# A state-space mixer with product-key experts: joint tap bursts, 16-bit column sums, and a fold remainder made once for two heads

## The chip, the cores and the metric

The kernel runs on one core of a Trainium2 chip. Its metric is the device time of one execution in microseconds (us), here the median of three runs. Five engines work side by side: TensorE (PE, with its weight loads shown apart as PEld), VectorE (DVE), ScalarE (ACT), GpSimd (POOL) and SyncE (SP), whose queue issues nearly all DMAs.

## The reference

```python
x = A_u                                             # (1, 2048, 576)
g = sigmoid((x * gate_w).sum(-1, keepdims=True))
# a: state-space convolution, one filter of 2048 taps per channel
dt = exp(log_dt)[:, None]; A = A_re + 1j * A_im
P = exp((dt * A)[:, :, None] * arange(L))           # (576, 128, 2048)
K = einsum("dn,dnl,dn->dl", Cc, P, dt * Bc).real
y = irfft(rfft(pad(u)) * rfft(pad(K)))[:L] + u * Dskip
# b: product-key experts, 32 heads, 64 x 64 experts, top 2
q = einsum("nd,dhc->nhc", xf, w_q); q1, q2 = q[..., :dk], q[..., dk:]
s1 = einsum("nhd,ed->nhe", q1, k1); s2 = einsum("nhd,ed->nhe", q2, k2)
# two best of s1 and of s2, two best of their four sums, softmax g over those
act = gelu(einsum("nd,nhkd->nhk", xf, u[top_e]))
out = einsum("nhk,nhk,nhkd->nd", g, act, v[top_e])
return g * a + (1 - g) * b
```

## The kernel before

All 2048 tokens stay on one core, in 16 tiles of 128. The Python code is a planner: it keeps a clock, an estimate of when each tile will be ready (`rdy`) and of when each engine is free, and lets generators (`spawn`, `ready`, `need`) run against it. What it emits is a fixed order of instructions for each engine; on the chip only data dependences and that order count. `mm` (line 213) emits every matmul and advances the clock by a cost given in the code, `Engine` (line 133) every operation of VectorE, ScalarE and GpSimd, `dma` (line 204) every DMA. PSUM has eight banks, dealt out under tags: `sc` (four, for scores, expert activations and outputs), `kb` (four while the taps are made) and `wb` (four afterwards).

The main loop at the end lays two kinds of long matmul groups on TensorE, 14 matmuls of 512 columns each: **s**, the scores of one token tile for eight sets of 64 keys (weights folded with the keys, `whl` and `wrem`), and **a**, the activations of 128 experts for 512 tokens (`uhl` and `wrem`). Every s tile goes to VectorE for the eight largest values and their indices. Between and inside these groups `pump()` lets the generators put their short matmuls in. fp32 values are taken as a high and a low 16-bit part (`split`), scaled by a power of two that `root_scale` makes from a bound on the column norms.

The parts that the change touches:

- **Column sums of squares.** A matmul with a matrix of ones adds 128 partitions. Where the squares are ScalarE's accumulated sums (`accum_out`, a column of `sc` in fp32), the ones are fp32 (`onesf`): `squares` (line 429, bank `sq`, two matmuls into one column, for each of eight blocks of 512 experts), `w_half` (line 478, bank `wn`, one matmul for each of 16 half groups of heads), `v_norm` (bank `pvn`, once) and `k_split` (bank `kn`, 128 columns, once, first of all). Where the squares are 16-bit already (`x_build`), the ones are `onesb`.
- **The fold.** For each group of four heads, in two halves, `w_half` waits for the query weights `w` (four sets of 576 rows), squares them on ScalarE into `junk`, makes the norm, and multiplies `w` by the keys `kt` in fp32, 64 rows of `w` at a time and two column tiles side by side (`wb`). 576 = 4 x 128 + 64, so four blocks of 128 rows go to `whl`, two to a bank, and the last 64 rows (the remainder, rows from 512 on) go into the third bank, computed for both halves of the partitions: eight matmuls with the same 64 rows twice. `w_tail` then takes each bank to its 16-bit parts; for the remainder ScalarE writes the high part of all 128 partitions in one operation of 256 elements, and VectorE the low part of the lower 64.
- **The taps.** 36 chunks of 16 channels run through `k_front` (phases, GpSimd and TensorE, reduction to a period), a joint exp and sin for two chunks on ScalarE, `k_gen` (products on GpSimd and VectorE for two chunks at a time) and a burst of 32 fp32 matmuls of 32-column tiles for each chunk into a bank `kb`. `kdone` counts finished chunks; `k_front(c)` starts once `kdone >= c - 3`, `k_gen(c)` once `kdone >= c`. `k_store` takes each chunk's bank to two fp16 parts, one ScalarE and one VectorE operation of 256 elements, into one half of `ko`; when both halves are there, one DMA stores them to `k_d`. After the last store `freq` starts: the taps are read back (`ksb`), transformed (`k_stage1`), multiplied by the transformed input (`products`: matmuls `pr`, `pi` and `pv`) and stored for the output stage.

After the taps and the frequency products comes the output stage: for each token tile `prep` builds one-hot matrices (`A`, `Be`, `Bg`) on VectorE, matmuls **S** spread the gate values over the experts, the result is multiplied by the gelu of the activations (`gl`) and split into `wh`, and matmuls **o** multiply `wh` by the experts' values `vhl`. The last 26 a groups are kept until all s groups are done and fill TensorE up to the first o. `gating` closes with transposes `tr` that the one-hots need.

## Time and profile before

| | |
|---|---|
| median of 3 runs | 1478.61 us (1476.39 to 1479.29) |
| the profiled execution | 1476.96 us, span 1475.2 us from first to last instruction |
| TensorE | 98% of the span, 14278 matmul records and as many weight loads |
| VectorE, ScalarE, GpSimd | 83%, 52%, 36% |
| DMA | 221.25 MB, mean 150 GB/s |
| granted TensorE clock | mean 0.999 |

In the profile an fp32 matmul stands as two records. Matmuls overlap: the end of one is modelled, and the step from one start to the next is what it costs in a stream. A group's line names the source line, engine, operation, output and inputs by the program's names, the shapes and the count, then busy us and mean ns of one, then the idle time of the engine before them and what ended it. A line of the timeline has the start and the time covered (us), and merges equal instructions that follow each other.

### The profile page before, as it was taken

To read this page: it belongs to the slowest core of one execution; us is meant where nothing else is said; L and a number is where in the kernel's file an instruction comes from. 1 tells how busy PE (TensorE), PEld (TensorE's weight loads), DVE (VectorE), ACT (ScalarE), POOL (GpSimd) and SP (SyncE) were. 2 spreads that over 40 slices of the span, in tenths; PEclk is the share of its full clock that TensorE was granted. 3 is DMA by queue.
4 is the path that set the end of the run, shared out by engine and by line. 5 is a ranking of instruction groups with operands and counts; after the bars stand their busy time and mean duration, and the time that the engine had idled before them with its cause. 6 is when DMAs were issued, how large, how long until landed. Compare 5 with 4: busy or idle time off the path is not lost.

```text
span 1475.2 us, 37349 instructions
## 1 busy us (share of the span) xinstructions
PE 1446.0 (98%) x14278; PEld 874.7 (59%) x14278; DVE 1224.1 (83%) x4590; ACT 770.9 (52%) x1276; POOL 535.5 (36%) x560
## 2 busy tenths in 40 slices
PE   6999999999999999999999999999999999999999
PEld 3445544455455554555555445456787788788787
DVE  6988899978988899577988897478998998898860
ACT  5557878677868776234555554665424324323310
POOL 0444636655456554002286999422010110110100
PEclk9999999999999999999999999999999999999999
DMA  6343433453344632656676846676532442441400
GB/s 235 124 126 117 149 106 107 147 180 97 122 120 129 191 102 83 193 205 222 232 255 206 278 157 201 205 230 182 190 124 96 129 144 69 152 146 67 154 10 17
DMA packets 139188, 221.25 MB, mean 150 GB/s; under 512 B 11648, under 2 KB 82688, under 8 KB 132608
## 3 DMA queue, kind: packets, MB, share of 16 engines
q1 hardware_dynamic: 138912, 218.78, 46.4%
q8 instruction: 112, 1.84, 0.5%
q14 instruction: 68, 0.56, 0.1%
q10 hardware_dynamic: 96, 0.07, 0.0%
HBM read 147.51 MB, written 71.30 MB: 148 GB/s over the span
## 4 chain that ended last, share of the span: by engine, by line
PE 74%; DVE 13%; DMA 4%; ACT 4%; POOL 2%; issue 2%; SPq 1%; DVEq 0%; ACTq 0%; POOLq 0%
PE o L213 22%; PE a L213 20%; PE s L213 18%; PE S L213 4%; PE wb L213 2%; DVE i L133 2%; PE kb L213 2%; DVE m L133 2%; PE pr L213 1%; SPq L204 1%; POOL vf L133 1%; PE y L213 1%; DVE uhl L133 1%; PE k L213 1%; DVE uh L133 1%
## 5 line engine op out<-in xcount | busy, mean ns | idle before, releaser
L213 PE MATMUL o<-vhl,wh 128*128 128x288 f16 x3072 | 387.3, 286 | 0.0
L213 PE MATMUL s<-whl,xb 128*128 128x512 f16 x1536 | 369.4, 381 | 4.8 <-DVE whl L133 2.5
L213 PE MATMUL a<-xb,uhl 128*128 128x512 f16 x1536 | 364.0, 379 | 0.0
L213 PEld LDWEIGHTS <-wh 128*128 128x128 f16 x3072 | 295.6, 98 | 76.7 <-issue 3.7
L213 PEld LDWEIGHTS <-xb 128*128 128x128 f16 x1792 | 170.5, 98 | 206.1 <-issue 17.1
L213 PEld LDWEIGHTS <-uhl 128*128 128x128 f16 x1536 | 147.5, 98 | 171.7 <-issue 2.1
L133 DVE FIND_INDEX8 i<-m,s 128x8 uint32<-128x64 f32 x1024 | 206.7, 224 | 0.0
L133 ACT ACTIVATE wh<-gl,s_wg 128x1024 f16<-128x1024 f32 x64 | 68.8, 1137 | 207.0 <-DVE gl L133 207.0
L133 DVE MAX8 m<-s 128x8 f32<-128x64 f32 x1024 | 146.3, 215 | 28.1 <-PE s L213 28.0
L133 POOL TENSOR_TENSOR CS<-CS,ex 128x512 f32<-128x512 f32 x72 | 100.5, 1427 | 179.7 <-DVE ex L133 179.7
L133 POOL TENSOR_TENSOR ya<-ya,db 128x576 f32<-128x576 f32 x16 | 32.0, 2009 | 333.8 <-DMA ya<-in_au_dram 183.1
L133 ACT ACTIVATE go<-a,i_a 128x512 f32<-128x512 f32 x93 | 63.3, 683 | 83.6 <-PE a L213 56.4
L133 DVE TENSOR_TENSOR gl<-S,gl 128x256 f32<-128x256 f32 x256 | 90.3, 417 | 16.7 <-PE S L213 10.2
L133 DVE SCALAR_TENSOR_TENSOR wh<-gl,s_wg,wh 128x1024 f16<-128x1024 f32 x64 | 92.0, 1468 | 12.9 <-ACT wh L133 12.8
L133 POOL TENSOR_TENSOR e<-aN,rt 128x512 f32<-128x512 f32 x72 | 83.8, 1183 | 18.4 <-PE kb L213 18.4
L133 DVE TENSOR_TENSOR Bg<-Be,vals 128x1024 f16<-128x1024 f16 x128 | 83.9, 697 | 2.2
L133 ACT ACTIVATE gl<-gl 128x1024 f32<-128x1024 f32 x64 | 63.5, 1045 | 41.3 <-DMA gl<-g_d 41.3
L133 DVE TENSOR_TENSOR A<-iota_a,vals 128x2048 f16<-128x2048 f16 x64 | 78.5, 1226 | 0.0
L213 PE MATMUL s<-wrem,xb 128*128 128x512 f16 x256 | 76.3, 380 | 0.4 <-DVE xb L133 0.4
L213 PE MATMUL a<-xb,wrem 128*128 128x512 f16 x256 | 76.2, 379 | 0.0
L213 PE MATMUL S<-Bg,A 128*128 128x64 f16 x2048 | 73.2, 193 | 2.1 <-DVE Bg L133 1.9
L213 PEld LDWEIGHTS <-A 128*128 128x128 f16 x2048 | 70.8, 97 | 7.3 <-issue 2.1
(206 smaller groups left out, 2233.6 us busy)
## 6 DMA issues: line engine op xcount, KB each, us to landing
g_d<-go SPq DMA_DIRECT2D x128, 256.0 KB, 2.5
gl<-g_d SPq DMA_DIRECT2D x32, 1024.0 KB, 5.4
wq<-in_wq_dram SPq DMA_DIRECT2D x16, 1152.0 KB, 7.6
us<-in_au_dram SPq DMA_DIRECT2D x64, 144.0 KB, 3.0
su_d<-us SPq DMA_DIRECT2D x32, 288.0 KB, 2.5
sk_d<-k1o SPq DMA_DIRECT2D x32, 288.0 KB, 2.9
vn<-in_vv_dram SPq DMA_DIRECT2D x32, 288.0 KB, 3.5
ui<-su_d SPq DMA_DIRECT2D x16, 576.0 KB, 4.0
```

Source lines behind the costliest of these rows:

```text
L133: return f(*a, **k)
L204: (q or DQ).dma_start(o, i)
L213: T.matmul(o, l, r, start=start, stop=stop)
```

## The change

- `onesf` is gone. All column sums use `onesb`; an fp32 value is read as the upper 16 bits of its word (`short`, `bitcast`). `squares` puts its two columns through one matmul and adds them on VectorE. `w_half` squares its four sets in two ScalarE operations of 1152 elements with a sum each, and adds both sums in two matmuls.
- The remainder's matmuls run once: the lower column tile takes sets 0 and 1, the upper one 2 and 3, four matmuls in place of eight. `w_tail` writes the high part in four ScalarE operations of 64 partitions and 128 elements, since both halves of the partitions need all four sets, and the low part in two on VectorE.
- `k_gen` waits for both chunks and puts them into one burst of 64 matmuls and one bank; `kdone` goes up by two. `k_store` runs once for two chunks, with 512 elements an operation.

```diff
--- before.py
+++ after.py
@@ -323,7 +323,6 @@
 
     cst = cp.tile([128, KT], F32, name="cst")
     ident, f2, fi = cst[:, 0:128], cst[:, 128:256], cst[:, 256:384]
-    onesf = cp.tile([128, 128], F32, name="onesf")
     onesb = cp.tile([128, 128], BF16, name="onesb")
     identb = cp.tile([128, 128], BF16, name="identb")
     halfpi = cp.tile([128, 1], F32, name="halfpi")
@@ -338,6 +337,10 @@
         col[again] += 1
         c = 96 + col[1] % 96 if again else col[0]
         return slice(c, c + 1)
+
+    def short(c0, n):
+
+        return sc[:, c0:c0 + n].bitcast(BF16)[:, 1:2 * n:2]
 
     def root_scale(bound2, margin, again=False):
 
@@ -435,10 +438,9 @@
         tag = side()
         yield from need(tag)
         p = bank(tag, "sq")
-        for n in range(2):
-            mm(p[:, 0:1], onesf, sc[:, acc[n]], n == 0, n == 1, 0.1)
+        mm(p[:, 0:2], onesb, short(acc[0].start, 2), True, True, 0.05)
         yield from ready(p)
-        V.tensor_copy(dst, p[:, 0:1])
+        V.tensor_reduce(out=dst, in_=p[:, 0:2], axis=AX, op=OP.add)
         free(tag, dst)
 
     def x_build(tb, a, r):
@@ -478,16 +480,18 @@
     def w_half(c, h, w):
         fl = lambda x: x.rearrange("p a b -> p (a b)")
         yield from ready(w)
-        acc = newcol(True)
-        junk = wj.tile([128, 4, D], BF16, tag="wj", name=f"wj{c}_{h}")
-        S.activation(fl(junk), fl(w), AF.Square, accum_out=sc[:, acc])
+        acc = newcol(True), newcol(True)
+        junk = wj.tile([128, 2, D], BF16, tag="wj", name=f"wj{c}_{h}")
+        for n in range(2):
+            S.activation(fl(junk), fl(w[:, 2 * n:2 * n + 2]), AF.Square, accum_out=sc[:, acc[n]])
         yield from ready(junk)
         while not sk:
             yield 0.3
         tag = side()
         yield from need(tag)
         p = bank(tag, f"wn{c}_{h}")
-        mm(p[:, 0:1], onesf, sc[:, acc], True, True, 0.1)
+        for n in range(2):
+            mm(p[:, 0:1], onesb, short(acc[n].start, 1), n == 0, n == 1, 0.03)
         yield from ready(p)
         s, i = root_scale(p[:, 0:1], kk, True)
         V.tensor_copy(invW[:, 2 * c + h:2 * c + h + 1], i)
@@ -505,12 +509,12 @@
             pbs.append((k, tag, bank(tag, f"wb{c}_{h}_{k}")))
         for k, tag, pb in pbs:
             for j in range(k, min(k + 2, 5)):
-                for g in range(4):
+                for g in range(4 if k < 4 else 2):
                     cs = slice(256 * (j - k) + 64 * g, 256 * (j - k) + 64 * g + 64)
                     rhs = kt[:, 64 * (g % 2):64 * (g % 2) + 64]
                     for hh in range(2):
-                        d = 128 * j + 64 * hh if k < 4 else 512
-                        mm(pb[64 * hh:64 * hh + 64, cs], w[:, g, d:d + 64], rhs, True, True, 0.06)
+                        gh, d = (g, 128 * j + 64 * hh) if k < 4 else (g + 2 * hh, 512)
+                        mm(pb[64 * hh:64 * hh + 64, cs], w[:, gh, d:d + 64], rhs, True, True, 0.06)
         for k, tag, pb in pbs:
             spawn(w_tail(c, k, pb, hl, rem, o, count, s, tag), 0.3 * k)
         del pb, pbs
@@ -528,10 +532,14 @@
             yield from split(hl[:, 0, k:k + 2, o], hl[:, 1, k:k + 2, o], pb.rearrange("p (k n) -> p k n", k=2), s)
             free(tag, hl)
         else:
-            S.activation(rem[:, 0, o], pb[:, 0:256], AF.Copy, scale=s)
+            halves2 = [(slice(64 * g, 64 * g + 64), slice(o.start + 128 * g, o.start + 128 * g + 128)) for g in range(2)]
+            for ps_, co in halves2:
+                for z in range(2):
+                    S.activation(rem[64 * z:64 * z + 64, 0, co], pb[ps_, 0:128], AF.Copy, scale=s[ps_])
             yield from ready(rem)
-            V.scalar_tensor_tensor(rem[0:64, 1, o], pb[0:64, 0:256], s[0:64], rem[0:64, 0, o],
-                                   op0=OP.mult, op1=OP.subtract)
+            for ps_, co in halves2:
+                V.scalar_tensor_tensor(rem[0:64, 1, co], pb[ps_, 0:128], s[ps_], rem[ps_, 0, co],
+                                       op0=OP.mult, op1=OP.subtract)
             free(tag, rem)
             free("hw", rem)
         count.append(k)
@@ -769,45 +777,37 @@
         calm[0] = 0
         if c + 2 < NCK:
             spawn(k_gen(c + 2))
-        for (d, CS, e, ex), Y in zip(both, Ys):
-            yield from ready(CS, Y, e)
-            yield 0.5
-            yield from need("kb")
-            kb = bank("kb", f"kb{d}")
+        yield from ready(*[x for (d, CS, e, ex), Y in zip(both, Ys) for x in (CS, Y, e)])
+        yield 0.5
+        yield from need("kb")
+        kb = bank("kb", f"kb{c}")
+        for m, ((d, CS, e, ex), Y) in enumerate(zip(both, Ys)):
             for i in range(NI):
                 for ri in range(2):
                     rhs_t = (Y, e)[ri]
                     for j in range(4):
                         n = NI * j + i
-                        mm(kb[32 * j:32 * j + 32, 64 * i:64 * i + 64], CS[:, n, 2 * ri, :], rhs_t[:, n, :],
+                        o = 64 * (NI * m + i)
+                        mm(kb[32 * j:32 * j + 32, o:o + 64], CS[:, n, 2 * ri, :], rhs_t[:, n, :],
                            ri == 0, ri == 1, 0.028)
-            kdone[0] += 1
-            spawn(k_store(d, kb))
-            del kb
-
-    kos = {}
+        kdone[0] += 2
+        spawn(k_store(c // 2, kb))
+        del kb
 
     def k_store(c, kb):
         yield from ready(kb)
-        if c % 2 == 0:
-            yield from need("ko")
-            take("ko", "ko")
-            kos[c // 2] = kg.tile([128, 2, 2 * NI * R2], F16, name="ko", tag="ko", bufs=1)
-        while c // 2 not in kos:
-            yield 0.2
-        ko = kos[c // 2]
-        kq = kb[:, :R2 * NI].rearrange("p (i q) -> p q i", i=NI)
-        kz = ko.rearrange("p z (q c i) -> p z c q i", c=2, i=NI)[:, :, c % 2]
+        yield from need("ko")
+        take("ko", "ko")
+        ko = kg.tile([128, 2, 2 * NI * R2], F16, name="ko", tag="ko", bufs=1)
+        kq = kb.rearrange("p (c i q) -> p q c i", c=2, i=NI)
+        kz = ko.rearrange("p z (q c i) -> p z q c i", c=2, i=NI)
         S.activation(kz[:, 0], kq, AF.Copy)
         yield from ready(ko)
         V.tensor_sub(kz[:, 1], kq, kz[:, 0])
         free("kb", ko)
         yield from ready(ko)
-        kstored[0] += 1
-        kos[c // 2, c % 2] = 1
-        if (c // 2, 1 - c % 2) not in kos:
-            return
-        dma(k_d[c // 2].rearrange("p z m q -> p z (m q)"), ko)
+        kstored[0] += 2
+        dma(k_d[c].rearrange("p z m q -> p z (m q)"), ko)
         free("ko", k_d)
         if kstored[0] == NCK:
             while uf != 0:
@@ -1250,7 +1250,7 @@
             tag = side()
             yield from need(tag)
             p = bank(tag, "pvn")
-            mm(p[:, 0:1], onesf, nut[:, 2:3], True, True, 0.1)
+            mm(p[:, 0:1], onesb, nut.bitcast(BF16)[:, 5:6], True, True, 0.05)
             yield from ready(p)
             sv.extend(root_scale(p[:, 0:1], 1.02))
             free(tag, sv[0])
@@ -1468,14 +1468,13 @@
     dma(cst, cst_d[:, :KT])
     xl = [x_load(0)]
     w_load(0, 1)
-    V.memset(onesf, 1.0)
     V.memset(onesb, 1.0)
     V.memset(halfpi, math.pi / 2)
     V.memset(magic, MAGIC)
     S.activation(halfpi, halfpi, AF.Copy)
     for w in wrems:
         V.memset(w[64:128, 1, :], 0.0)
-    ksq = vals[:, 0].rearrange("p g k -> p (g k)")
+    ksq = vals[:, 0].rearrange("p g k -> p (g k)").bitcast(BF16)[:, 0:128]
 
     def k_split():
         yield from ready(kt)
@@ -1483,7 +1482,7 @@
         yield from ready(ksq)
         yield from need("kb")
         p = bank("kb", "kn")
-        mm(p[:, :128], onesf, ksq, True, True)
+        mm(p[:, :128], onesb, ksq, True, True)
         yield from ready(p)
         V.tensor_reduce(out=kk, in_=p[:, :128], axis=AX, op=OP.max)
         free("kb", kk)
```

## The prediction

> **What bounds the kernel now.** I read the page first, then the list of what TensorE waited for, then a table of stages, then the timeline of TensorE around each piece that the change touches.
>
> ```profile
> span 1475.2 us, 37349 instructions
> PE 1446.0 (98%) x14278; PEld 874.7 (59%) x14278; DVE 1224.1 (83%) x4590; ACT 770.9 (52%) x1276; POOL 535.5 (36%) x560
> ```
>
> TensorE (PE) has work in flight for 1446.0 of 1475.2 us; the next engine, VectorE (DVE), for 1224.1. The waits of PE from 30 us on (who waited for whom: total us, times, longest) are ten rows that add up to 12.3 us; four and the last of them:
>
> ```profile
> PE k L213 <- ACT k1o L133: 2.3, 1, 2.3
> PE sq L213 <- ACT uhl L133: 2.0, 3, 1.5
> PE S L213 <- DVE Bg L133: 1.9, 5, 0.5
> PE s L213 <- DVE xb L133: 1.9, 3, 1.0
> ...
> PE kP L213 <- DVE CS L133: 0.2, 1, 0.2
> ```
>
> By stage (length, then busy PE, weight loads, DVE, ACT, POOL): taps, frequency products, hand-over to the output stage.
>
> ```profile
> 150.00:595.00 445.00, 444.12 (x4568) 227.31 (x4557) 399.32 (x1497) 331.80 (x481) 240.99 (x198) 1.00 0.42 126
> 732.00:935.00 203.00, 199.87 (x1969) 101.94 (x1964) 168.80 (x1077) 103.75 (x288) 170.00 (x224) 1.00 0.64 216
> 935.00:1017.00 82.00, 81.45 (x648) 41.60 (x647) 54.66 (x100) 56.69 (x94) 19.41 (x15) 1.00 0.69 224
> ```
>
> The granted clock is 1.00 in all three. While the taps are made, PE is without work for 0.9 us in 445: score and expert products fill whatever the tap chain leaves. So a matmul taken away shortens the run by the step it took from the next one's start, as long as the other engines keep up; their busy time there (DVE 399 of 445) leaves room, but not much.
>
> **The change part by part.** Start-to-start steps count, not durations, since matmuls overlap.
>
> The sums of squares. Each fp32 matmul leaves two records.
>
> ```profile
> 275.00 1.24 PE L213 MATMUL s<-whl,xb 128*128 128x512 f16 x5
> 276.08 0.28 PE L213 MATMUL wn<-sc,onesf 128*128 128x1 f32 x2
> 276.22 0.59 PE L213 MATMUL s<-wrem,xb 128*128 128x512 f16 x2
> 357.60 0.50 PE L213 MATMUL sq<-sc,onesf 128*128 128x1 f32 x4
> 358.03 0.32 PE L213 MATMUL kb<-Y,CS 128*32 128x64 f32 x8
> 976.15 1.13 PE L213 MATMUL S<-Bg,A 128*128 128x64 f16 x32
> 977.12 0.81 PE L213 MATMUL a<-xb,uhl 128*128 128x512 f16 x3
> ```
>
> Five s matmuls take 276.08 - 275.00 = 1.08 us, a step of 0.216. One `wn` holds PE for 0.14 us, a `sq` (two fp32 matmuls) for 0.43, of which 0.09 is the entry into the four-tile shape that follows (below), so 0.34. The nearest row for a small 16-bit matmul with its own 128x128 weights is S: 32 in 0.97 us, 0.030 each. It has 64 columns where these have one or two, so I take 0.03, with 0 and the 0.14 of now as ends. `wn` becomes two such: 0.14 - 0.06 = 0.08, in 14 places (the first two lie in the start, counted there): 1.1 us. `sq` becomes one: 0.31 in 7 places: 2.2 us. The one `pvn` gives 0.1. `kn` lies in the first 4 us, where PE waits for data anyway: 0. At the other end, 0.14 for each new matmul, `wn` would lose 14 x 0.14 = 2.0 and `sq` gain 7 x 0.2 = 1.4. The Trainium skill (TensorE: Matmul & The Clock Gate, Back-to-back issue gap) has a rule that speaks against this part: a stream of weight load and matmul pairs with 128 columns is said to go at about 81 ns a pair. By that estimate the two parts together would give about 1.8 us where I count 3.3. The S rows, 30 ns, disagree with it for 64 columns; no row shows one column.
>
> The remainder of the fold. The burst falls from 40 matmuls to 36, 80 records to 72.
>
> ```profile
> 301.75 0.60 PE L213 MATMUL a<-xb,wrem 128*128 128x512 f16 x2
> 302.27 2.55 PE L213 MATMUL wb<-kt,wq 128*64 128x64 f32 x80
> 304.76 0.61 PE L213 MATMUL a<-xb,uhl 128*128 128x512 f16 x2
> ```
>
> From the burst's start to the next matmul is 2.49 us; about 0.12 of it is the turn back to full tiles (as in the next rows), so a record costs 2.37/80 = 0.030, eight 0.24, and in 14 bursts 3.3 us.
>
> One burst for two chunks.
>
> ```profile
> 160.41 0.81 PE L213 MATMUL a<-xb,uhl 128*128 128x512 f16 x3
> 161.15 0.32 PE L213 MATMUL kb<-Y,CS 128*32 128x64 f32 x8
> 161.29 0.29 PE L213 MATMUL kb<-e,CS 128*32 128x64 f32 x8
> ...
> 161.84 0.30 PE L213 MATMUL kb<-Y,CS 128*32 128x64 f32 x8
> 161.96 0.29 PE L213 MATMUL kb<-e,CS 128*32 128x64 f32 x8
> 162.18 0.60 PE L213 MATMUL a<-xb,uhl 128*128 128x512 f16 x2
> ```
>
> Without a change of tile shape the burst would start at 160.41 + 3 x 0.216 = 161.06; it starts at 161.15, 0.09 later. Its eight groups stand 0.14, then six times 0.112, then 0.22 apart. A single burst costs 1.12 us, a joint one 0.09 + 0.14 + 14 x 0.112 + 0.22 = 2.02, against 2.24 for two: 0.22 x 18 = 4.0 us.
>
> Sum on PE: 1.1 + 2.2 + 0.1 + 3.3 + 4.0 = 10.7 us gone.
>
> Beside PE the change adds instructions to ScalarE (ACT) and VectorE (rows: busy total, mean ns).
>
> ```profile
> L133 ACT ACTIVATE wj<-wq 128x2304 bf16<-128x2304 f32 x16 | 33.9, 2121 | 9.8 <-DMA wq<-in_wq_dram 9.8
> L133 ACT ACTIVATE uhl<-us 128x2048 bf16<-128x2048 f32 x8 | 15.3, 1907 | 3.9 <-DMA us<-in_uT_dram 3.9
> L133 ACT ACTIVATE whl<-wb,sci 128x512 f16<-128x512 f32 x20 | 13.6, 684 | 28.3 <-PE wb L213 27.0 <-DVE sci L133 1.2
> L133 ACT ACTIVATE wrem<-wb,sci 128x256 f16<-128x256 f32 x16 | 7.4, 465 | 1.6 <-PE wb L213 1.6
> L133 ACT ACTIVATE uhl<-ur 128x512 bf16<-128x512 f32 x8 | 5.0, 622 | 0.0
> L133 ACT ACTIVATION_READ_ACCUMULATOR wj<-wq 128x1 f32 x16 | 3.1, 195 | 0.0
> L133 DVE TENSOR_TENSOR ko<-kb,ko 128x256 f16<-128x256 f32 x36 | 15.0, 416 | 0.2
> L133 DVE SCALAR_TENSOR_TENSOR wrem<-wb,sci,wrem 64x256 f16<-64x256 f32 x16 | 7.5, 467 | 0.3 <-ACT wrem L133 0.3
> ```
>
> Squares: 622 at 512 elements and 1907 at 2048 give 0.84 ns an element, so 1152 cost 1.16 us; two and one more accumulator read are 2.32 + 0.20 against 2.12: +0.4 us for each of 16 halves. Remainder: 465 at 256 and 684 at 512 give 0.86 ns an element, 0.36 us at 128; four are 1.42 against 0.465: +0.96 us for each of 16; VectorE pays two of about 0.36 for one of 0.467, +0.25. The Trainium skill (VectorE: DVE Perf Modes, The TRN2 errata) warns against just this: the fixed cost is paid by every instruction, so many small pieces lose. Its table for reading PSUM gives as an estimate four times 0.25 us against 0.36, +0.64 where the rows give +0.96. The store does the reverse: 18 subtractions of 512 elements for 36 of 256 save VectorE some 3 us by the fixed part of the rows. All told ACT gains some 20 us in 1475 while it is 52% busy, and VectorE changes by under 2 us. From 30 us on s and a matmuls cover this, a fold being due several us before its first use: I cost it at 0 there. If that cover is gone, a fold's tail is 1.2 us later in each of seven heads' groups: 8 us.
>
> At the start nothing covers it.
>
> ```profile
> 14.24 0.47 ACT L133 ACTIVATE wrem<-wb,sci 128x256 f16<-128x256 f32 x1 [0.92 <-PE wb L213]
> 20.97 1.24 ACT L133 ACTIVATE whl<-wb,sci 128x512 f16<-128x512 f32 x2
> 24.58 4.22 PE L213 MATMUL s<-whl,xb 128*128 128x512 f16 x11 [2.51 <-DVE whl L133]
> ```
>
> ACT runs from 14.24 on almost without a break. The first remainder (+0.96) and the second half's squares (+0.4) lie ahead of the whl pair, which moves from 20.97 to about 22.3 and ends at 23.6. In the order of the changed program VectorE now takes both remainder pieces ahead of the last low part of whl; they wait for four ACT pieces (25.0), take 0.65, and that part 0.75: 26.4 in place of 24.58, so +1.8 us. Ends: -0.4 (fold and small matmuls alone) and +2.5.
>
> New waits: the planner deals the whole order anew. Ten rows gave 12.3 us before; I allow 1 us more, with -3 and +9 as ends. Joining makes the first chunk wait for the second, and `kdone` goes up in twos, so the front of the next even chunk starts later. I counted the matmuls of both orders at the steps above: the last tap burst stands 10 us of PE work later than before, the last back-product 12 us later, the first output matmul 10.5 us earlier.
>
> Sum: -10.7 + 1.8 + 1.0 = -7.9 us on the profiled 1476.96 us (span 1475.2 and 1.8 around it). The median of the runs, 1478.61, stands 1.65 above that run, so I forecast 1478.61 - 7.9 = 1470.7 us.
>
> **The rivals.**
>
> *All of it arrives.* The start costs nothing and no wait is added: -10.7, 1467.9 us. For it: PE idles 0.9 us in the 445 of the taps. Against: the start's ACT chain.
>
> *The hand-over starves PE (slower).* The side chain from the last back-product to the first output matmul is one-hots, S, products with the gated activations, wh.
>
> ```profile
> 934.68 0.33 PE L213 MATMUL pv<-vf,cst 64*64 64x192 f32 x2
> 964.37 1.22 DVE L133 TENSOR_TENSOR A<-iota_a,vals 128x2048 f16<-128x2048 f16 x1
> 1017.35 3.10 PE L213 MATMUL o<-vhl,wh 128*128 128x288 f16 x24
> ```
>
> Before it had 1017.35 - 934.68 = 82.7 us, filled by a matmuls; the changed order has 59 us of PE work there. If the chain needed all 82.7, PE would stand for 23.7 us: 1470.7 + 23.7 = 1494.4. It turns the result to slower from a stall of about 11 us on. Against it: the first one-hot stood at 964.37 because the transposes came after the last back-product, and in the new order they come before it; from the first one-hot to the first o were 53 us, and if it follows the last back-product by 6 us, 53 remain. That is enough with nothing to spare, so a few us are likelier than 24.
>
> *The gain is dealt away.* Waits spread over the stages grow by the +9 end, as in the fold's cover of 8 us: -10.7 + 1.8 + 9 = 0.1, 1478.7 us. For it: VectorE's 399 of 445 and a new order. Against: the same planner costs the same operations, and left 0.9 us there.
>
> That the change does not do what it says is hardly open: the built program has 18 joint bursts and 36 fold matmuls in each half. Only the step of a one-column matmul is unseen.
>
> **How the numbers follow.** Forecast 0.58, all arrives 0.16, dealt away 0.14, hand-over 0.12. The last holds both signs of "much" and "little": a stall of 3 us belongs to the forecast. The forecast's own range is 1467 to 1475. The low end of the whole goes to 1465 (all arrives and 3 us of today's waits go); the high end takes in the dealt-away case: 1480. A measurement of this kernel can tell about 0.2%, 3 us, from no change, so faster means under 1475.6 and slower over 1481.6: faster 0.75, same 0.13, slower 0.12.
>
> **What would show it.** Right: 18 tap bursts of about 2.0 us, folds of 72 records in about 2.25, `sq` and `wn` at 0.03 a matmul; the second run of s at 26 us; o starting some 8 us earlier; PE waits after 30 us near 13 us. Wrong: one-column matmuls at 0.1 or more, a PE wait on Bg, wh or vhl of over 5 us near 960 to 1000, or waits of s on whl at each head.

## The result, and the profile after

The changed kernel took 1482.63 us (median of 7 runs, 1481.82 to 1485.6) against 1478.61 for the kernel before: a ratio of 1.0034, with a 95% interval of 1.0023 to 1.0046. It is slower by 4.0 us, 11.9 us above the forecast of 1470.7 and 2.6 us above the upper end of the range. The profiled execution took 1482.38 us, at a mean granted clock of 0.994 (before 0.999). The page after:

```profile
span 1480.6 us, 37067 instructions
PE 1436.8 (97%) x14120; PEld 866.3 (59%) x14124; DVE 1244.0 (84%) x4590; ACT 794.8 (54%) x1335; POOL 550.5 (37%) x561
```

TensorE is busy for 9.2 us less than before, in a span that is 5.4 us longer: it stands idle for 43.8 us where it stood for 29.2. VectorE has as many instructions as before, 4590, and is busy for 19.9 us more. The table of stages (length, then busy PE, PEld, VectorE, ScalarE, GpSimd, then the granted clock; the stage of the taps is shown up to 606 us, though their last burst stands at 618 in this order) shows where:

```profile
150.00:606.00 456.00, 444.69 (x4417) 226.75 (x4407) 416.35 (x1573) 335.72 (x496) 246.52 (x194) 0.99 0.40 125
735.00:935.00 200.00, 197.39 (x1912) 100.96 (x1911) 163.71 (x997) 108.54 (x306) 159.50 (x218) 1.00 0.70 236
935.00:1017.00 82.00, 81.80 (x657) 40.57 (x656) 53.30 (x89) 52.19 (x80) 30.09 (x29) 1.00 0.68 224
1017.00:1480.00 463.00, 452.75 (x5185) 364.33 (x5184) 377.52 (x596) 137.85 (x142) 38.07 (x21) 1.00 0.35 112
```

While the taps are made, TensorE idles for 456.00 - 444.69 = 11.3 us, where it idled 0.9 in 445 us before. The stretch from 935 to 1017, in which a hand-over rival would have shown, idles 0.2. What TensorE waited for from 30 us on (total, times, longest):

```profile
PE a L213 <- DVE i L133: 4.0, 2, 2.5
PE y L213 <- ACT vhl L133: 3.8, 1, 3.8
PE S L213 <- DVE Bg L133: 3.5, 5, 1.5
PE kb L213 <- DVE i L133: 2.7, 1, 2.7
PE u L213 <- DVE uh L133: 2.2, 2, 1.5
...
PE u L213 <- DVE i L133: 0.3, 1, 0.3
```

The twelve rows add up to 22.4 us, where ten gave 12.3 before; 15.9 of it names VectorE. None of the waits of before of 2 us and more (`k` on `k1o`, `sq` on `uhl`) is among the large ones, and none of these five but `S` on `Bg` stood there: they are other waits in other places.

The timeline of TensorE shows that the edits themselves came out as they were costed. A joint burst with a fold behind it, a `sq` and a `wn`:

```profile
313.83 0.81 PE L213 MATMUL a<-xb,uhl 128*128 128x512 f16 x3
314.57 0.32 PE L213 MATMUL kb<-Y,CS 128*32 128x64 f32 x8
314.71 0.29 PE L213 MATMUL kb<-e,CS 128*32 128x64 f32 x8
...
316.27 0.29 PE L213 MATMUL kb<-e,CS 128*32 128x64 f32 x8
316.50 2.32 PE L213 MATMUL wb<-kt,wq 128*64 128x64 f32 x72
318.75 2.12 PE L213 MATMUL a<-xb,uhl 128*128 128x512 f16 x9
...
334.38 0.17 PE L213 MATMUL sq<-sc,onesb 128*128 128x2 bf16 x1
334.40 0.59 PE L213 MATMUL s<-wrem,xb 128*128 128x512 f16 x2
...
407.45 0.19 PE L213 MATMUL wn<-sc,onesb 128*128 128x1 bf16 x2
407.50 0.59 PE L213 MATMUL s<-wrem,xb 128*128 128x512 f16 x2
```

The burst takes 316.50 - 314.57 = 1.93 and the 0.09 of its entry, 2.02 us; the fold's 72 records 2.25; `sq` holds TensorE for 0.02 us and a pair of `wn` for 0.05.

To set work and waits apart I price every start-to-start step of TensorE at the mean step of the same pair of matmuls where nothing disturbs it. A step of 0.45 us or more counts as a wait above that price, and what steps take above it while the granted clock is at half is counted by itself (the lower five rows are experiments, told below; the last two are one kernel, run twice):

| kernel (profiled execution) | span | work at clean steps | waits | extra at half clock |
|---|---|---|---|---|
| before | 1475.2 | 1440.6 | 26.0 | 1.7 |
| after | 1480.6 | 1426.4 | 41.1 | 6.3 |
| joint_alone | 1475.9 | 1437.6 | 29.3 | 2.1 |
| sums_rem_old_order | 1471.4 | 1430.7 | 29.7 | 3.9 |
| sums_rem_kb_order | 1468.6 | 1431.1 | 27.0 | 3.7 |
| full_in_joint_order | 1476.4 | 1426.6 | 37.2 | 5.7 |
| full_in_joint_kb_order | 1476.5 | 1426.4 | 36.2 | 7.0 |

From before to after the work falls by 14.2 us; waits of 15.1 and half-clock time of 4.6 more give it back, and more. The experiments ask whether these waits belong to the edits or to what the planner dealt.

### The profile page after: what moved, and what is told of

The parts are those of the page before. It is cut to its first block, busy times and chain, and to the rows that moved or that the text cites. A ratio compares the mean times of both kernels' runs of the same rounds, so it can differ in the third digit from the quotient of the medians.

```text
span 1480.6 us, 37067 instructions
## 1 busy us (share of the span) xinstructions
PE 1436.8 (97%) x14120; PEld 866.3 (59%) x14124; DVE 1244.0 (84%) x4590; ACT 794.8 (54%) x1335; POOL 550.5 (37%) x561
## 4 chain that ended last, share of the span: by engine, by line
PE 77%; DVE 17%; ACT 2%; DMA 2%; issue 1%; SPq 0%; DVEq 0%; ACTq 0%
PE o L213 23%; PE a L213 20%; PE s L213 19%; PE S L213 4%; DVE i L133 3%; PE wb L213 2%; PE pr L213 2%; DVE m L133 2%; DVE e L133 2%; PE kb L213 2%; PE y L213 1%; DVE Y L133 1%; DVE CS L133 1%; DVE uhl L133 1%; DVE wh L133 1%
## 5 line engine op out<-in xcount | busy, mean ns | idle before, releaser
L133 DVE SCALAR_TENSOR_TENSOR wh<-gl,s_wg,wh 128x1024 f16<-128x1024 f32 x63 | 91.5, 1483 | 11.3 <-ACT wh L133 11.3
L133 ACT ACTIVATE go<-a,i_a 128x512 f32<-128x512 f32 x98 | 66.5, 683 | 54.8 <-PE a L213 42.2
L133 DVE TENSOR_TENSOR Bg<-Be,vals 128x1024 f16<-128x1024 f16 x128 | 89.0, 737 | 2.2
```

What stands on the lines that cost most here:

```text
L133: return f(*a, **k)
```

## The experiments

**Each edit by itself.** Three kernels take one part of the diff each, and leave the planner free to deal: the joint burst with its store (hunks `k_gen`, `k_store`), the 16-bit sums (`squares`, `w_half`, `pvn`, `kn`), the remainder (`w_half`'s fold, `w_tail`).

> Only the joint burst and store for two chunks. All theories: 18 bursts take 4.0 us of steps off TensorE. Theory 'joint burst waits' (a burst that needs both chunks stands where the second chunk is late, and TensorE is in order): waits of TensorE while the taps are made grow by some 10 us as in the changed kernel, about 1483 us. Theory 'dealt order' (any edit makes the planner deal another order, whose waits are a matter of chance): waits anywhere between 1 and 12 us, 1472 to 1484. Theory 'extra pieces' (the added ScalarE and VectorE instructions are what is late): no added pieces here, so 1474.5.

> Only the 16-bit column sums, with the squares of the query weights in two operations. Work taken off TensorE: 3.4 us. 'Joint burst waits': 1475 to 1476. 'Dealt order': anywhere from 1470 to 1486, the waits while the taps are made differing from the 1.1 us of before. 'Extra pieces': half of them are here (16 more ScalarE squares), so about 1479 or more.

> Only the remainder of the fold made once. Work taken off TensorE: 3.3 us and about 0.5 in the two first folds. 'Joint burst waits': 1475 to 1476, the start 1 us longer. 'Dealt order': anywhere from 1470 to 1486. 'Extra pieces': 48 more ScalarE and 16 more VectorE instructions, waits of s on whl at the heads, 1480 or more.

Measured: 1479.95 us (ratio 1.0014, 1.0004 to 1.0024), 1489.57 (1.007, 1.0057 to 1.0083) and 1487.34 (1.0071, 1.0052 to 1.0089). Every part that takes work off TensorE is slower alone, two of them more than all together. With the sums alone TensorE waits for `S` on `Bg` in the output stage, 10.2 us in all with a longest of 5.8, a stage that this edit does not touch:

```profile
PE S L213 <- DVE Bg L133: 10.2, 7, 5.8
PE o L213 <- POOL vhl L133: 2.1, 1, 2.1
```

**The same work, dealt differently.** If an edit acts through the order, the kernel before must move without any edit. The planner's own numbers are changed, one at a time. TensorE's matmuls stay the same, all 14278 records of them. The planner also gives some operations to whichever engine it believes free (`if S.free <= V.free`), so in the last three of these kernels 32 to 49 of the 6426 operations of VectorE, ScalarE and GpSimd change their engine along with the order. What is tested is the deal, order and engine together.

```diff
-    spawn(k_params(), 30)                                   # before_redealt_31
+    spawn(k_params(), 31)
-            mm(p[:, 0:1], onesf, sc[:, acc[n]], n == 0, n == 1, 0.1)   # before_dealt_sq
+            mm(p[:, 0:1], onesf, sc[:, acc[n]], n == 0, n == 1, 0.14)
-        mm(p[:, 0:1], onesf, sc[:, acc], True, True, 0.1)
+        mm(p[:, 0:1], onesf, sc[:, acc], True, True, 0.14)
-                           ri == 0, ri == 1, 0.028)         # before_dealt_kb
+                           ri == 0, ri == 1, 0.031)
-        t = 0.085 + 0.00083 * size(out)                      # before_dealt_act
+        t = 0.095 + 0.00083 * size(out)
```

> The kernel before with one number of the planner changed: the taps' parameters are started at 31 us of its clock in place of 30. The same instructions in another order. 'Dealt order': TensorE's work stays within 1 us, its waits move by several us, the time by 3 us or more, either way but more likely up, since the order before has only 1.1 us of waits in the taps. 'Joint burst waits' and 'extra pieces': nothing that they name is here, so within 2 us of 1478.6.

> The kernel before with one cost of the planner changed (the sums of squares at 0.14 us a matmul in place of 0.1): the same instructions, but the order on TensorE parts from that of before after 126 of 4131 stretches and agrees with it in 87 of 100 of them, as little as the changed kernel's does. (The run with 31 for 30 had kept TensorE's order almost whole, so it tested nothing.) 'Dealt order': work within 1 us of before, waits of TensorE and half-clock time up by 5 to 15 us, time 1482 to 1492. 'The edits themselves' (their extra waits and pieces): none is here, so within 2 us of 1478.4.

> The kernel before with the planner's cost of a tap matmul at 0.031 us in place of 0.028: the same instructions, the order agrees in 88 of 100 stretches. 'Dealt order': waits up by 5 to 15 us, 1482 to 1492. 'The edits themselves': within 2 us of 1478.4.

> The kernel before with the planner's fixed cost of a ScalarE operation at 0.095 us in place of 0.085: the same instructions, the order agrees in 89 of 100 stretches. 'Dealt order': 1482 to 1492. 'The edits themselves': within 2 us of 1478.4.

Measured: 1477.97 us (0.9998, 0.9989 to 1.0006; the order hardly changed, so this run says nothing), 1503.21 (1.0167, 1.0152 to 1.0183), 1476.33 (0.9991, 0.998 to 1.0002) and 1486.0 (1.0049, 1.0035 to 1.0063). The same work lies 27 us apart, and the worst of the four comes from charging these matmuls nearer to what they take (0.14 us a `wn`, 0.17 each of two `sq`). Its output stage, and what TensorE waited for there:

```profile
1017.00:1499.00 482.00, 458.88 (x5190) 367.74 (x5188) 388.45 (x605) 148.16 (x158) 43.88 (x25) 0.98 0.36 113
```

```profile
PE S L213 <- DVE Bg L133: 12.3, 6, 4.4
PE o L213 <- POOL vhl L133: 5.3, 2, 2.8
PE S L213 <- DVE ya L133: 3.1, 1, 3.1
```

23.1 us idle in that stage, against 1475 - 1017 - 451.44 = 6.6 in the kernel before. The dealing alone is worth more than the whole change.

**The change, dealt once more.** The changed kernel with its tap matmuls charged at 0.031 for 0.028.

> The changed kernel with the planner's cost of a tap matmul at 0.031 us in place of 0.028: its instructions, another order (91 of 100 stretches agree with it). 'Dealt order': waits move by several us against the changed kernel's 41, 1472 to 1488. 'The edits themselves': within 2 us of 1482.6, with some 10 us of waits in the taps again.

Measured: 1483.36 us (1.003, 1.0016 to 1.0044), so a second deal of the changed kernel is slower too. Its three product groups on VectorE (below) take 107.6 us, so that the figure of 114 us, which the expectation of joint_bank_two_bursts gives for three traces, holds for two of them.

**Sums and remainder with every other instruction in its place.** The planner is charged what the old instructions cost, while the new ones are emitted; the matmul groups of TensorE then follow each other in the order of the kernel before.

```diff
-            self.free = start + self.cost(op, out, a, k)
+            self.free = start + (held.pop(0) if held else self.cost(op, out, a, k))
...
+        held.extend((0.085 + 0.00083 * 2304 + 0.15, None))   # w_half: two squares charged as one
...
-            mm(p[:, 0:1], onesb, short(acc[n].start, 1), n == 0, n == 1, 0.03)
+            mm(p[:, 0:1], onesb, short(acc[n].start, 1), n == 0, n == 1, 0.1 * (n == 0))
...
+            held.extend((0.085 + 0.00083 * 256 + 0.07, None, None, None))   # w_tail: four pieces as one
```

> The 16-bit sums and the remainder made once, but the planner is charged the old costs for them, so that every other instruction stands where it stood before, on all engines. The joint burst is left out. 'Dealt order' (the edits are good by what they take off TensorE, and only the order that the planner dealt beside them lost it): 3.4 + 3.3 us less work, the start -0.5 to +1.8, waits elsewhere within 2 us of before: 1471 to 1474. 'The edits themselves' (the added ScalarE and VectorE pieces come late): 1479 or more, as each of the two alone.

> The same two edits in the order of the run before_dealt_kb (1476.3 us). 'Dealt order': 5 to 7 us under that, 1469 to 1472. 'The edits themselves': 1477 or more.

Measured: 1472.53 us (0.9954, 0.9941 to 0.9966) in the order of before, and 1470.41 (0.995, 0.9937 to 0.9963) in that of before_dealt_kb. Alone and dealt anew the same two edits had cost 0.7% each; in place they bring 0.46%, 6.8 us. The prediction had 6.7 us for them on TensorE. The second has the lowest median found, not clear of the first; both beat the two kernels of the change.

**The joint burst, taken apart.** While the taps are made VectorE multiplies each chunk's phases (`Y`, then `e` twice). The three groups before, and after:

```profile
L133 DVE TENSOR_TENSOR Y<-e,CS 128x1024 f32<-128x1024 f32 x36 | 44.6, 1238 | 0.0
L133 DVE TENSOR_TENSOR e<-e,CS 128x512 f32<-128x512 f32 x36 | 26.4, 733 | 3.3
L133 DVE SCALAR_TENSOR_TENSOR e<-e,CS 128x512 f32<-128x512 f32 x36 | 26.4, 732 | 0.0
```

```profile
L133 DVE TENSOR_TENSOR Y<-e,CS 128x1024 f32<-128x1024 f32 x36 | 49.2, 1368 | 4.7 <-PE kb L213 4.7
L133 DVE TENSOR_TENSOR e<-e,CS 128x512 f32<-128x512 f32 x36 | 32.7, 908 | 3.4 <-ACT wb L133 0.5
L133 DVE SCALAR_TENSOR_TENSOR e<-e,CS 128x512 f32<-128x512 f32 x36 | 32.2, 896 | 0.0
```

The same 108 instructions take 114.1 us for 97.4, most of VectorE's 19.9 more. Two kernels were to tell whether this is what TensorE waits for: one keeps the joint bank and store but issues the two bursts apart (`kdone` by one), the other is the joint burst with the next fronts held back until its products are under way.

```diff
+            kdone[0] += 1                 # joint_bank_two_bursts: in the loop, after each chunk's burst
-        kdone[0] += 2
...
+        if c + 3 in kf:                   # joint_products_first
+            calm[0] = 1
         kdone[0] += 2
```

> Joint_alone with its burst taken apart again: one bank and one store for two chunks, but each chunk's 32 matmuls follow when that chunk is ready, and kdone goes up by one each time. In the three traces with a joint burst VectorE needs 114 us for the products Y and e of the taps, against 94 to 100 in all traces without. 'Collision' (kdone going up by two starts GpSimd's next front at the moment at which VectorE makes the next pair's products, and both slow each other): back to 94 to 100 us, TensorE's waits in the taps under 5 us; the time then 1473 to 1490 by the deal. 'Dealt order alone': Y and e not tied to the burst, anything from 94 to 115.

> Joint_alone with one line more: when the next pair's factors are there, the fronts are held back (calm) until its products are on their way, so GpSimd's front work comes after VectorE's Y and e. 'Collision': Y and e fall from 114 to under 102 us with the joint burst kept; the taps end later, since the fronts start later, by some 5 us a pair at most. 'Dealt order alone': Y and e stay anywhere, no tie to this line.

Measured: 1485.14 us (1.0038, 1.0025 to 1.0051) and 1482.49 (1.0026, 1.0015 to 1.0037). Products took 102.9 us in the first and 93.2 in the second; waits and half-clock time between 150 and 600 us were 11.0 and 7.9 (before 1.1, joint burst alone 8.7). The second is the answer: with the products below their old price, 7.9 us remain, and 6.5 of them are `u` waiting for `uh` on VectorE. The slow products are real, but the waits do not need them.

**The full change in held orders.** Sums and remainder are charged at the old costs as above, the joint burst is made as in the change, with a tap matmul charged at 0.028. The second run was meant to charge 0.031. Its kernel.py, though, has 0.028 and is the first one's to the byte, so it is the same kernel run again, and the order that its expectation speaks of has not run.

> All edits of the change, with the same instructions as the changed kernel, but the planner is charged the old costs for the sums and the remainder, so that every other instruction keeps the place that it has in the kernel with the joint burst alone (1479.95 us). Theory 'the orders are what gives the gain back': sums and remainder bring what they brought in the old order of before (a ratio of 0.9954, 6.8 us), 1473 us (1471 to 1475), some 9 us faster than the changed kernel on the same instructions; the waits of TensorE stay near the 29 us of the joint burst alone. Rival 'the edits together cost it' (joint burst, sums and remainder get in each other's way on VectorE or ScalarE): 1480 to 1484 us, as the changed kernel, with waits near 41 us.

> The same, but the order dealt with a tap matmul charged at 0.031 for 0.028 throughout, joint burst included, so another order of the same instructions. Theory 'the orders': within 1466 to 1478 us, since the joint burst has not run in this order; below 1470.4, the best so far, if the joint burst's 4 us arrive, above it if its waits in the taps (8.7 us against 1.1) come back. Rival 'the edits together cost it': 1480 to 1484 us here too.

Measured: 1478.89 us (1.0008, 0.9999 to 1.0017) and, the same kernel again, 1478.39 (0.9999, 0.9988 to 1.001): between both theories of the first. The waits, 37.2 and 36.2 us, did not stay near 29. On the work of the changed kernel the deal is worth 0.26 to 0.35% (1.0034 against 1.0008 and 0.9999), 4 to 5 us. But adding the joint burst to sums and remainder turned 0.9954 into 1.0008 and 0.9999, about 0.5%, 7 to 8 us. In the tally it takes 4.1 and 4.3 us off TensorE's work, as it should, and brings 9.3 and 9.6 of waits and half-clock time. Between 150 and 600 us, first in sums_rem_old_order, then in full_in_joint_order:

```profile
150.00:600.00 450.00, 447.92 (x4593) 226.80 (x4583) 405.80 (x1552) 338.86 (x508) 242.34 (x201) 1.00 0.42 126
```

```profile
150.00:600.00 450.00, 439.28 (x4541) 223.62 (x4542) 404.83 (x1331) 342.51 (x495) 255.82 (x199) 1.00 0.44 133
```

2.1 us idle became 10.7. VectorE is no busier in that stretch; GpSimd is, by 13.5 us.

**Which part of the joint burst.** On sums and remainder with held costs, one part each: `kdone` in twos; one bank and store; the first burst waiting for both chunks.

```diff
-            kdone[0] += 1                 # sums_rem_fronts_in_twos
+            kdone[0] += 2 * (d % 2)
...
+            if not m:                     # sums_rem_one_store: bank taken once, k_store of the change
+                kb = bank("kb", f"kb{c}")
...
+        yield from ready(*[x for (d, CS, e, ex), Y in zip(both, Ys) for x in (CS, Y, e)])   # sums_rem_burst_waits_for_both
+        yield 0.5
         for (d, CS, e, ex), Y in zip(both, Ys):
-            yield from ready(CS, Y, e)
-            yield 0.5
```

> Sums and remainder charged at the old costs (1472.5 us in the old order), and of the joint burst only the count: kdone goes up by two after the second chunk's burst, so the front of the next even chunk starts later; bursts, banks and stores stay one for each chunk. The full change, charged in the same way, took 1478.9 us, with 14.5 us of waits and half-clock time on TensorE between 150 and 600 us against 2.6. Theory 'the later front starves VectorE's share of the tap chain': waits of over 8 us in that stretch and 1478 to 1484 us. Rival 'the bank and store do it, or only the order dealt': waits under 5 us and 1470 to 1476 us.

> The same, and of the joint burst only the one bank for two chunks with one store of 512 elements; the bursts stay apart, and kdone goes up by one. Theory 'the shared bank and store do it' (a bank held over two bursts, one longer operation on VectorE and on ScalarE): waits of over 8 us between 150 and 600 us, with the longest behind ko or kb, and 1478 to 1484 us. Rival 'the later front does it': under 5 us there and 1470 to 1476 us. If this run and the one with the fronts in twos both have over 8, it is neither part but the order that either deals.

> The same, and of the joint burst only the wait: both bursts are issued when both chunks are ready, with a bank and a store for each, and kdone going up by one after each. Theory 'the wait for the second chunk does it': waits of over 8 us between 150 and 600 us, 1478 to 1484 us. Rival: in the profile before, the two bursts of a pair stood 0.7 us apart, so that this wait is hardly one: under 5 us there and 1469 to 1476 us; with bursts that follow each other closely some of the 4 us of the joint burst should arrive too.

Measured: 1485.94 us (1.0058, 1.0042 to 1.0073), 1486.08 (1.0061, 1.0044 to 1.0078) and 1473.15 (0.9973, 0.9963 to 0.9983). The first two came out above both of their expected ranges. Waits and half-clock time between 150 and 600 us: 5.4, 16.9 and 5.8 us. So the wait for the second chunk is cleared of most of the loss. One store has its waits among the taps, as its theory said; the longest stands behind `ko` on VectorE, 3.0 us. The fronts in twos have 5.4 there, and their largest loss elsewhere, in `S` on `Bg` in the output stage (7.4 us). Each of these two parts alone costs more than the whole joint burst does on the same base, so they don't add up as prices would.

**What sums and remainder bring in place.** Four pairs of these kernels have the same matmul groups on TensorE in the same order, but for the matmuls of sums and fold themselves. So each pair prices these two edits with everything else in its place:

| without | with both edits | ratio to before | waits and half-clock time, 150 to 600 us |
|---|---|---|---|
| before | sums_rem_old_order | 1 to 0.9954 | 1.1 to 2.6 |
| before_dealt_kb | sums_rem_kb_order | 0.9991 to 0.995 | 0.2 to 0.4 |
| joint_alone | full_in_joint_order (and again) | 1.0014 to 1.0008 (0.9999) | 8.7 to 14.5 (13.0) |
| joint_bank_two_bursts | sums_rem_one_store | 1.0038 to 1.0061 | 11.0 to 16.9 |

In the first two orders TensorE hardly waits while the taps are made, and the edits bring 0.4 to 0.5%. In the other two it waits already, and they bring 0.15% at most, or a loss, though from joint_alone to full_in_joint_order TensorE's work falls by 11.0 us. One place shows how, first in joint_alone, then in full_in_joint_order:

```profile
171.85 0.50 PE L213 MATMUL sq<-sc,onesf 128*128 128x1 f32 x4
172.22 0.41 PE L213 MATMUL u<-uh,tu 128*128 128x288 f16 x2
```

```profile
172.56 0.17 PE L220 MATMUL sq<-sc,onesb 128*128 128x2 bf16 x1
173.08 0.42 PE L220 MATMUL u<-uh,tu 128*128 128x288 f16 x2 [0.35 <-DVE CS L139]
```

The step from `sq` to `u` was 0.37 us. With the cheap `sq` it is 0.52, and 0.35 of that is a wait for VectorE: here the work taken away stood in front of a wait, and the wait took its place.

## Why the prediction was wrong

The step that failed is "New waits: I allow 1 us more, with -3 and +9 as ends". It measured 15.1 us of waits and 4.6 of half-clock time, with the start's share in it. The argument behind the 1 us was that ten rows of waits gave 12.3 us before, as if that were a property of the kernel and its planner. It was a property of one deal, and a good one: kernels with the same work, dealt differently, lay between 1476.3 and 1503.2 us. VectorE's 399 of 445 us, which the prediction had as its warning, does not tell a good deal from a bad one: before_dealt_kb has 409.11 of 450 and TensorE idles 0.1 us there, before_dealt_act has 394.82 and TensorE idles 4.0. With this step fell the one behind the sum, "a matmul taken away shortens the run by the step it took": it held in the two orders without waits (0.46 and 0.41%) and not in the two with them (0.15% at most, and a loss). The rival "the gain is dealt away" named the right mechanism, with a chance of 0.14 and a price of 9 us. The price was half of what it had to be. Of the three kernels with the same work that were dealt anew, two lost 7 us and more, so the chance was too small as well.

The result can be split by the experiments' ratios to the kernel before: sums and remainder with everything else in place, -0.46%; the joint burst on top of them, planned with the same charges, +0.54%; the planner's own charges and so its own deal for all three, +0.26%. They add up to the measured +0.34% because each starts where the last one ends, so the sum is no proof. The split depends on its order, too: the joint burst first is +0.14%, sums and remainder in its order -0.06%, the planner's own charges again +0.26%. By its own steps the prediction had -0.33% (6.7 us less 1.8 of the start), -0.27% (4.0 us) and +0.07% (the 1 us of waits) for these three.

How a wait arises shows best in the timeline. After, VectorE at 250 us and, with GpSimd idle, at 429 us, then GpSimd and TensorE at 250:

```profile
249.49 0.69 DVE L133 TENSOR_TENSOR e<-e,CS 128x512 f32<-128x512 f32 x1
250.10 0.69 DVE L133 SCALAR_TENSOR_TENSOR e<-e,CS 128x512 f32<-128x512 f32 x1
250.70 0.23 DVE L133 COPY ex<-ex 128x2 f32<-128x2 f32 x2
250.96 3.67 DVE L133 SCALAR_TENSOR_TENSOR uh<-us,sci,uh 64x576 f16<-64x576 f32 x2
...
429.29 0.82 DVE L133 SCALAR_TENSOR_TENSOR uh<-us,sci,uh 64x576 f16<-64x576 f32 x1
```

```profile
251.01 6.42 POOL L133 TENSOR_TENSOR CS<-CS,ex 128x512 f32<-128x512 f32 x4 [13.89 <-DVE ex L133]
```

```profile
249.83 1.67 PE L213 MATMUL s<-whl,xb 128*128 128x512 f16 x7
253.04 0.41 PE L213 MATMUL u<-uh,tu 128*128 128x288 f16 x2 [1.53 <-DVE uh L133]
```

The small copy at 250.70 releases GpSimd's products; the two `uh` that follow on VectorE run beside them and take 3.67 us, where one takes 0.82 us at 429.29; TensorE's next matmul in order is the `u` that needs them, and it stands for 1.53 us with s and a groups behind it that could have run. The joint burst alone has the same picture at 199.57 (two `uh` in 3.67 us) and TensorE there waits for 2.09 us. The planner's formula charges a `uh` 0.67 us (0.07 + 576 x 0.00104), and 0.55 more where it believes GpSimd at work: 1.22 at most, for the 1.84 that each took here. But all 32 `uh` take 45.0 us before and 44.7 after: the collision costs as much in both. So what seems to have changed is whether TensorE's order has something else in front of the matmul that needs the result; no run shows that by itself. The Trainium skill (SBUF — State Buffer, Who interferes with whom) says that a VectorE instruction with two SBUF inputs contends with a GpSimd instruction that reads SBUF; the 0.82 and the 3.67 us agree. In this trace each `uh` that takes over 0.82 us ends 0.6 to 0.7 us after the GpSimd instruction that was running when it began (spans on GpSimd are rough).

The other steps, in the prediction's order:

- *The small sums, 0.03 us a matmul.* Right: 0.02 and 2 x 0.025. The 81 ns that the prediction quoted as a rule against this part is not what these matmuls show. Its estimate by that rule, 1.8 us, is `sq` alone; with `wn`, which loses 0.3 us by it, it is 1.5.
- *The fold, 0.24 us each; the joint burst, 2.02 us.* Right to 0.01 us: 2.25 and 2.02. Of the 14.2 us in the tally 10.7 were predicted, and the two folds, two `wn` and one `sq` of the start, at the same steps, are about 1 more; 2 to 3 us are not assigned.
- *The start, +1.8.* The second run of s, and the run behind the next `wrem` (29.07 us before), after and in sums_rem_old_order:

```profile
25.36 4.50 PE L213 MATMUL s<-whl,xb 128*128 128x512 f16 x11 [3.50 <-DVE whl L133]
...
30.13 2.75 PE L213 MATMUL s<-whl,xb 128*128 128x512 f16 x12
```

```profile
24.39 4.85 PE L220 MATMUL s<-whl,xb 128*128 128x512 f16 x11 [2.37 <-DVE whl L139]
...
29.70 2.75 PE L220 MATMUL s<-whl,xb 128*128 128x512 f16 x12
```

After, the second run starts 0.8 later than before and the next one 1.1, not 1.8; with both edits that lengthen ScalarE's chain, in the old order, they are 0.2 earlier and 0.6 later. So in that order ScalarE's added pieces do not hold up the second run. The rest goes with the clock: it was at half for 3.4 us from 24.9 us on before, and for 6.8 us in both of these kernels, from 22.5 and 22.7 on.
- *ScalarE's 20 us are covered.* Busy time rose by 23.9 us. In the order of before, with the same pieces, the gain of sums and remainder arrived, so their cover held there.
- *VectorE changes by under 2 us.* Wrong: 19.9, most of it from the products beside GpSimd's fronts. joint_products_first, without that slowing, still has 7.9 us of waits and half-clock time in the taps (joint_alone 8.7).
- *Moves.* The last tap burst stands 25 us later than before (10 predicted), the last back-product 24 (12 predicted), and the first o at 1019.75 us, 2.4 later, where 8 to 10.5 earlier was predicted. The hand-over nevertheless did not starve TensorE: from 959.0 to 1019.75 the chain took 61 us, well under the 82.7 that the rival would have needed.

What stays open is why a joint burst goes with more waits among the taps in all its orders (7.9 to 16.9 us between 150 and 600 us in seven kernels with the joint burst or its bank; of eleven without, ten have 5.8 or less and one 8.5). The wait for the second chunk is not it. The bank with its store and the fronts in twos are not told apart from the orders that they deal, since no kernel here has them with every other instruction in its place. A joint burst in the order of before_dealt_kb, where TensorE waits least, has not been run either.

## What to carry to other kernels

Where a planner deals the order, a change of cost is a change of order for the whole program, and its price is drawn from the spread of deals: measure that spread first, by moving the planner's numbers with the work as it is, and forecast with it. Judge an edit with the order held, by charging the planner the old cost, and in more than one order, since in place the same edits brought 0.46% in one and nothing in another; then deal anew, several times, and keep the best. An engine that is never waited for in one order may be waited for in the next, so a stage with 0.9 us of idle time shows a well-dealt order and not slack.

## What the runs showed of the hardware

Short waits of TensorE can cost more than themselves. In joint_alone a wait of 2.09 us is followed by s matmuls at full clock; in full_in_joint_order the same place has 2.59 us, and three s matmuls behind it cover 1.02 and then 1.48 us:

```profile
201.64 0.40 PE L213 MATMUL u<-uh,tu 128*128 128x288 f16 x2 [2.09 <-DVE uh L133]
...
202.77 0.81 PE L213 MATMUL s<-whl,xb 128*128 128x512 f16 x3
203.66 0.81 PE L213 MATMUL s<-whl,xb 128*128 128x512 f16 x3
```

```profile
203.36 0.40 PE L220 MATMUL u<-uh,tu 128*128 128x288 f16 x2 [2.59 <-DVE uh L139]
203.60 1.02 PE L220 MATMUL s<-whl,xb 128*128 128x512 f16 x3
...
204.90 1.48 PE L220 MATMUL s<-whl,xb 128*128 128x512 f16 x3
```

The granted clock is at half for 3.4 us there, from 204.1 on. After has three such stretches behind waits (213.7, 254.7 and 1039.7 us) where before has none past the start. The Trainium skill (TensorE: Matmul & The Clock Gate, What's actually happening) describes a clock that halves after an idle window of about 3.4 us that runs freely; the stretches are as long as that window, but waits of 2.6 us and less in one piece were enough here (2.59 in full_in_joint_order; 1.53 and 0.66 within 2 us, ahead of 254.7 in after). A wait's length alone does not decide it: one of 2.51 us in after, at 584 us, was followed by full clock, and the kernel of full_in_joint_order had two such stretches past the start in one profile and three in the other.
